# Transfers of weights, values, queries and keys issued at other places of a group and a round; one early sum before small steps; two calls on VectorE moved

## The chip, the cores and the metric

The program runs on one core of a Trainium2 chip. A core has a matrix engine (TensorE, PE in the profile; its weight loads are listed as PEld), a vector engine (VectorE, DVE), a scalar engine (ScalarE, ACT), a general engine (GpSimd, POOL) and a sync engine (SyncE, SP). Each runs its own list of instructions in order, and they wait for one another through semaphores. SP computes nothing: it holds one queue of DMA issues, and an issue whose semaphores have not arrived holds up every issue behind it. ACT and POOL issue some DMAs of their own. The on-chip memory is SBUF, 128 partitions wide; products of PE land in PSUM and are read from there by DVE and ACT. The metric is the device time of one execution in microseconds (us), lower is better.

## The reference

A layer norm of x feeds two branches: a local attention, in which each of 2048 positions looks at itself and at seven earlier ones two apart, and a bilinear feed-forward network. The result is x plus the attention's output times the SiLU of the network's output. In the core of the reference:

```
x = A_x                                     # 1 x 2048 x 640, float32
xn = layernorm(x)
qkv = xn @ wqkv                             # 640 x 1920, 32 heads of 20
idx = pos[:, None] - 2 * arange(8)          # negative ones masked
attn = softmax(einsum(q, k[idx]) * 20**-0.5)
s = einsum(attn, v[idx]) @ wo               # 640 x 640
h = (xn @ w_gate) * (xn @ w_up)             # two 640 x 1536
out = x + s * silu(h @ w_down)              # 1536 x 640
```

## The kernel before

**Products.** Every product keeps float32 accuracy from three passes in a reduced type: each operand is split into a high part (a copy by ACT, L109) and a low part (the operand minus its high part, L110, on POOL unless DVE is named), and PE adds high by high, high by low and low by high. From the feed-forward's column block 3 on, a block of 128 hidden columns is computed for two chunks of 512 positions by seven half-size products in place of eight (a Winograd scheme); the sums and differences that this needs are made on POOL and DVE. `group(f, c0, second)` (L1287) does it for block f and one pair of chunks; its products are called j and come in the order 0, 5, 2, 1, 4, 3, 6 (the place in this order is n). After a product, ACT copies it to SBUF into one of five rotating buffers `gh` (`hold`, L1295); DVE and POOL combine them (L1298 `gate_b`, L1301 `up_b`, L1304 `h_b`, L1308 `gate_a`, L1311 `up_a`), and SP stores two finished tiles h to the DRAM scratch h_scr (L1284). A hold reuses a buffer only once the last reader of it is done: that is L1304 on POOL, or the landing of a store of h.

**The stages.** Up to about 60 us: layer norm, queries, keys and values of the first head groups, first feed-forward blocks. For the norm, `scales` (L278 to L281, L331 to L334, tiny operations on POOL) makes the factors of eight tiles, and PE multiplies them out (L340) for the use by the next transposes; on POOL they stand among `early_sums` (L593), eight sums of 128x512 for the first chunks' Winograd operands, which are stored in t_scr and e_scr and not read before the groups. Up to about 290 us: the remaining queries, keys and values, each stored to qkv_scr by ACT's queue. From 290 to 515 us: two groups for each block, 3 to 10 in f. Then the last block's plain products (`gate`, `up`, L1354 to L1372), and the output projection of the attention: `pair_product` (L1021), seven products again, for pairs of o tiles, which `load_pair` reads from o_scr, `turn_pair` (L976) turns by four 32x32-block transposes (L710, shown as two for each pair) and combines by four sums (L982 to L985), and `hi_pair` (L1008) and `lo_pair` (L1012) split. After 540 us: the down projection and the end.

**The attention** runs on DVE and POOL alone, beside all this, as a generator (`attention`, L461) which yields an estimate of what a step costs and is advanced a little after each product of PE: what stands in which order on an engine is set by these calls and the estimates, in program order. A unit n is one group of heads with one parity of positions. Its 8 offsets are done two at a time (four rounds j = 0, 2, 4, 6): DVE multiplies q by two shifted keys (L527) and sums over the head's columns (L534), and between these, for the unit before, DVE multiplies weights by values (L498) and POOL adds the result up (L504). After the four rounds the sums of the unit before are stored in o_scr by SP (L575), and a softmax of unit n follows (L549 to L563; the exponential is ACT's, L556). Queries (L408), keys and values (L414 and L416, the last ones shifted by a partition) are loaded by SP, keys and values in two alternating buffers `kv`. `ahead(n, parts)` issues the load of unit n's queries and keys (part 0) or of its values (part 1) once, if they have been computed by then.

**SP's queue** is thus shared by the stores of h, the stores of o, the loads of q, keys and values, and the load of a block's raw weights (`load_wf`, L175, 640 KB, in two alternating buffers `wraw`), in program order. Of a block's weights POOL makes the sums (L1272) and the splits (L110) while the block before is multiplied.

Of the kernel before, what the change touches and what calls it, by code (L numbers as in the profile page):

```python
# [43 lines left out]
PAIRS = range(0, W, 2)  # L44
PACE = 1.0
VEC = 3
EARLY = 3
GROUP_RATE = 0.184


# [6 lines left out]
def kernel(  # L57
# [115 lines left out]
    def load_wf(f):  # L173
        wf_raw[f] = slot([P, KD, 2, P], F32) if f == 0 else st([P, KD, 2, P], "wraw", 2)
        nc.sync.dma_start(wf_raw[f], wgu[f])  # L175
# [285 lines left out]
    def attention():  # L461

        def flat(y):
            return y.rearrange("p i c -> p (i c)")

        terms = st([P, 2, NE * CMAX], "t", 2)
        twice = st([P, 2, NE * CMAX], "t", 2)
        spots = NE * W
        m_ps = weights[0:1, CH - spots:].rearrange("p (i w) -> p i w", w=W)
        nc.vector.tensor_copy(m_ps, mask)  # L470
        before, loaded = None, set()

        def ahead(n, parts):

            if n < len(ORDER) and ORDER[n] in made:
                for a in parts:
                    if (n, a) not in loaded and ORDER[n]:
                        loaded.add((n, a))
                        (load_kq if a == 0 else lambda u: load_kv(u, 1))(ORDER[n])

        copied = set()

        def copy_q(n):

            if n not in copied:
                copied.add(n)
                y = flat(q_t[ORDER[n]])
                nc.scalar.activation(q_two[:, :y.shape[1]], y, AF.Copy)

        def values(w):  # L490

            u, e, o = before
            nh = GROUPS[UN[u][0]]
            c = nh * DH
            y = flat(o)
            t = terms[:, w % 2, :NE * c]
            v = flat(kv_t[u][:, 1, w:w + NE, :]).rearrange("p (n d) -> p n d", d=DH)
            nc.vector.tensor_mul(t.rearrange("p (n d) -> p n d", d=DH),  # L498
                                 e[:, :, w].unsqueeze(2).to_broadcast([P, NE * nh, DH]), v)
            eng, cost = (nc.gpsimd, 1.3e-3) if u != ORDER[-1] else (nc.gpsimd, 2.2e-3) if w % 2 else (nc.vector, 2.5e-3)  # L500
            if w == 0:
                return NE * c * cost, lambda: None
            z = terms[:, 0, :NE * c] if w == 1 else y
            return NE * c * cost, lambda: eng.tensor_add(y, z, t)  # L504

        ring[:] = [q_one, "g", "u"]
        for n, u in enumerate(ORDER + [None]):
            if u is not None:
                late_unit = u not in made
                while u not in made:  # L510
                    yield None
                ahead(n, (0, 1))
                for _ in range(5 if late_unit else 0):
                    yield None
                g, r = UN[u]
                nh = GROUPS[g]
                c = nh * DH
                copy_q(n)
                q, kv = q_two[:, :NE * c].unsqueeze(1).to_broadcast([P, 2, NE * c]), kv_t[u]
                lg = st([P, NE * nh, W], "lg", 2)  # L520
                t = twice.rearrange("p a c -> p (a c)")[:, :2 * NE * c].rearrange("p (a c) -> p a c", a=2)
            for j in PAIRS:
                if u is not None:
                    ahead(n + 1, (0,))
                    k = flat(kv[:, 0, j:j + NE, :])
                    k = bass.AP(k.tensor, k.offset, [k.ap[0], [c, 2], k.ap[1]])
                    nc.vector.tensor_mul(t, q, k)  # L527
                    yield 2 * NE * c * 1.22e-3
                if before is not None:
                    cost, add = values(j)  # L530
                    add()
                    yield cost
                if u is not None:
                    nc.vector.tensor_reduce(out=lg[:, :, j:j + 2].rearrange("p n a -> p a n"),  # L534
                                            in_=t.rearrange("p a (n d) -> p a n d", d=DH), op=ALU.add, axis=AX.X)
                    yield 2 * NE * c * 1.2e-3
                if before is not None:
                    cost, add = values(j + 1)
                    add()
                    yield cost  # L540
            if u is None:
                store_o(before)
                ring[:] = three
                return
            ahead(n + 1, (0, 1))
            if before is not None:
                store_o(before)
            m0 = lg[0:1].rearrange("p (i h) w -> p i h w", h=nh)
            nc.vector.tensor_add(m0, m0, m_ps.unsqueeze(2).to_broadcast([1, NE, nh, W]))  # L549
            e = weights[:, :NE * nh * W].rearrange("p (n w) -> p n w", w=W)  # L550
            most = weights[:, CH - spots - NE * nh:CH - spots]
            sm = st([P, 2, NE * nh], "sm", 1)
            nc.vector.tensor_reduce(out=most, in_=lg, op=ALU.max, axis=AX.X)
            nc.vector.tensor_sub(lg, lg, most.unsqueeze(2).to_broadcast([P, NE * nh, W]))
            yield 1.5
            nc.scalar.activation(e, lg, AF.Exp, scale=SCALE)  # L556
            if (n + 1, 0) in loaded:
                copy_q(n + 1)
            finish_piece()
            yield 0.5  # L560
            nc.vector.tensor_reduce(out=sm[:, 0, :], in_=e, op=ALU.add, axis=AX.X)
            nc.vector.reciprocal(sm[:, 1, :], sm[:, 0, :])
            nc.vector.tensor_mul(e, e, sm[:, 1, :].unsqueeze(2).to_broadcast([P, NE * nh, W]))  # L563
            before = u, e, st([P, NE, c], "o", 1)
            yield 1.3
# [42 lines left out]
    def advance(budget):  # L608
        credit[0] += budget
        while running and credit[0] > 0:  # L610
            cost = next(running[0], 0)
            if cost == 0:
                running.pop()
            elif cost is None:
                break
            else:
                credit[0] -= cost
        if credit[0] > 0:
            credit[0] = 0
# [72 lines left out]
    def split_wo(k, eng=nc.gpsimd):  # L692
        y = slot([P, 2, D])
        hi, lo = y[:, 0], y[:, 1]
        split(eng, wo_raw.pop(k), hi, lo)
        wo_s[k] = hi, lo
# [540 lines left out]
    def two(f):  # L1237
        return F_TWO <= f < f1
# [48 lines left out]
    def group(f, c0=0, second=0):  # L1287
# [26 lines left out]
        if not second:  # L1314
            if not two(f - 1):
                w_split(f, "U")
            w_sum.pop(f, None)
            wf_raw.pop(f)
            if f < f1 and f + 1 not in wf_raw:
                load_wf(f + 1)  # L1320
        for n, j in enumerate((0, 5, 2, 1, 4, 3, 6)):
            y = b["ACACABA"[j]]
            runs = [(w_unit(f, H_IN[j], k)[i], x_in(W_IN[j], l, k, c0)) for i, l in ALL3 for k in range(2)]
            if j in FIVE:
                name, ch = FIVE[j]
                runs += [(w_unit(f, name)[i], xT[c0 + ch][l][:, KD - 1, :]) for i, l in ALL3]
            for r, (w, x) in enumerate(runs):
                nc.tensor.matmul(y, w, x, start=j in (0, 1, 5) and r == 0, stop=r == len(runs) - 1,  # L1328
                                 skip_group_check=True)
            if j in (0, 1, 2, 4):  # L1330
                hold(j)
            finish_piece()
            for act in later:
                act()
            later = {5: [gate_a], 3: [gate_b, up_b]}.get(j, [])
            if j == 6:
                unfinished.extend([up_a, h_b])
            if (second, n) in places:
                places[second, n](f)
            if (f, second, n) in beside:  # L1340
                beside[f, second, n]()
            advance(PACE * len(runs) * (GROUP_RATE if two(f) else 0.184))

    places = {}
# [54 lines left out]
    for m, t in ((m, t) for m in range(1, len(MADE)) for t in range(DIL)):  # L1399
# [23 lines left out]
        elif (m, r) == (last, 1):  # L1423
            for k in range(2):
# [3 lines left out]
    w_sum.pop(2)  # L1428
    load_wf(3)
    beside.update({(f0, 0, 5): lambda: advance(1e9), (f0, 1, 0): lambda: begin_last(), (f0, 1, 1): lambda: load_pair(0),  # L1430
                   (f0, 1, 4): lambda: sums_wo(), (f0, 1, 5): lambda: split_wo(0, nc.vector),
                   (f0, 1, 6): lambda: split_wo(1, nc.vector)})

    def begin_last():
        advance(1e9)
# [66 lines left out]
    split_wo(3)  # L1502
    split_w5()
    g3 = gate(f1, 3)
    turn_pair(2)
    up(f1, 3, g3)
    finish_piece()
    begin_wd()
# [23 lines left out]
    for p in range(SP // 2):  # L1532
# [6 lines left out]
        if more:  # L1539
            hi_pair(p + 1, 0)  # L1540
            lo_pair(p + 1, 0)
            if p == 3:
                wd_sums()
        else:
            split_o(SP, y1)
# [129 lines left out]
```

## Time and profile before

| | us |
|---|---|
| median of three runs | 748.99 |
| lowest, highest | 748.61, 751.39 |
| the profiled execution | 748.28 |
| its span | 746.5 |

The profiled execution thus has 1.8 us outside its span, and it ran 0.7 us faster than the median.

| engine | busy us | share of span | instructions |
|---|---|---|---|
| PE | 735.4 | 99% | 4054 |
| DVE | 612.2 | 82% | 720 |
| POOL | 462.6 | 62% | 389 |
| ACT | 302.5 | 41% | 577 |

The rows of a timeline read: start, duration, engine, source line, operation, output<-input, count, and in brackets how long the engine was idle before and what ended that. A row with a count (x2) stands for neighbouring instructions; its duration is theirs together. A row of DMA issues ends with the KB of one and the median time in us from issue to landing. The list of waits names an engine, the bank and line that waited, the engine and line that it waited for, the total in us, how often, and the longest. The table of stretches shows for each engine the busy time and, in brackets, the instructions; then the TensorE clock that was granted, the share of the DMA engines and GB/s.

### The profile page before, as it was taken

What the parts mean: (1) busy time and instruction counts of PE and PEld (TensorE: products, weight loads), DVE (VectorE), ACT (ScalarE), POOL (GpSimd) and SP (SyncE); (2) the same over time, 40 slices, a digit from 0 to 9 for tenths busy, and PEclk for the clock granted to TensorE, in tenths of its full rate; (3) what the DMA queues carried; (4) which work ended last, traced back from release to release, by engine and by line L of the source; (5) the groups of instructions that cost most, each with busy time, mean ns of one, the idle gap of its engine ahead of it and who ended that gap; (6) DMA issues with size and microseconds to landing.
All of it is one profiled execution on the core that took longest, in us unless ns stands there. A gap on an engine that the chain in (4) does not pass through costs nothing. (4 is left out here: it accounts for less than half of the span.)

```text
span 746.5 us, 11102 instructions
## 1 busy us (share of the span) xinstructions
PE 735.4 (99%) x4054; PEld 669.0 (90%) x4054; DVE 612.2 (82%) x720; ACT 302.5 (41%) x577; POOL 462.6 (62%) x389
## 2 busy tenths in 40 slices
PE   8999999999999999999999999999999999999997
PEld 6989989988999998778887888887899999999997
DVE  7666998699697887998999999667998777777775
ACT  5658413323332332233223322335556564444442
POOL 6169929787688878888879989877559800000000
PEclk9999999999999999999999999999999999999999
DMA  9465672947446548856165424268567655555534
GB/s 316 170 202 200 236 224 87 299 157 239 127 152 197 190 128 232 274 161 207 55 159 149 115 82 110 72 178 204 167 177 212 228 220 191 191 191 191 191 106 141
DMA packets 103493, 132.98 MB, mean 178 GB/s; under 512 B 22696, under 2 KB 74404, under 8 KB 103438
## 3 DMA queue, kind: packets, MB, share of 16 engines
q1 hardware_dynamic: 84686, 112.77, 48.4%
q10 hardware_dynamic: 17600, 14.26, 5.9%
q0 software_dynamic: 1152, 5.24, 2.2%
q8 instruction: 32, 0.52, 0.3%
q14 instruction: 23, 0.19, 0.1%
HBM read 83.58 MB, written 47.81 MB: 176 GB/s over the span
## 5 line engine op out<-in xcount | busy, mean ns | idle before, releaser
L504 POOL TENSOR_TENSOR o<-o,t 128x960 f32<-128x960 f32 (+1 forms) x69 | 139.6, 2024 | 19.1 <-DVE t L498 17.6
L498 DVE TENSOR_TENSOR t<-e,kv 128x960 f32<-128x960 f32 (+1 forms) x96 | 99.4, 1037 | 24.8 <-POOL o L504 24.7
L527 DVE TENSOR_TENSOR t<-q,kv 128x1920 f32<-128x1920 f32 (+1 forms) x48 | 92.4, 1925 | 4.3 <-DMA kv<-qkv_scr 4.2
L534 DVE TENSOR_REDUCE lg<-t 128x96 f32<-128x1920 f32 (+1 forms) x48 | 92.3, 1922 | 0.2
L428 PE MATMUL q<-s,xc 128*128 128x360 f32 (+1 forms) x450 | 83.1, 334 | 0.6 <-DVE lg L266 0.5
L110 POOL TENSOR_TENSOR s<-wraw,s 128x384 fp32r<-128x384 f32 (+6 forms) x58 | 69.6, 1210 | 19.9 <-ACT s L109 19.9
L428 PEld LDWEIGHTS q<-s,xc 128*128 128x128 f32 x450 | 74.9, 188 | 4.8 <-DVE lg L266 0.8
L1295 ACT ACTIVATE gh<-g 128x512 f32<-128x512 f32 x54 | 32.2, 597 | 115.8 <-PE g L1328 97.8
L428 PE MATMUL u<-s,xc 128*128 128x360 f32 (+1 forms) x360 | 65.8, 334 | 0.0
L428 PEld LDWEIGHTS u<-s,xc 128*128 128x128 f32 x360 | 60.3, 188 | 2.3
L428 PE MATMUL g<-s,xc 128*128 128x360 f32 (+1 forms) x330 | 61.5, 337 | 0.0
L428 PEld LDWEIGHTS g<-s,xc 128*128 128x128 f32 x330 | 55.7, 188 | 2.6
L1328 PE MATMUL u<-xc,s 128*128 128x512 f32 x216 | 55.3, 391 | 0.9 <-ACT gh L1295 0.9
L896 PE MATMUL q<-xc,s 128*128 128x320 f32 x342 | 55.5, 309 | 0.0
L1328 PE MATMUL g<-s,s 128*128 128x512 f32 x216 | 55.0, 390 | 0.0
L896 PEld LDWEIGHTS q<-xc,s 128*128 128x128 f32 x342 | 51.5, 188 | 0.0
L1328 PEld LDWEIGHTS u<-xc,s 128*128 128x128 f32 x216 | 40.3, 188 | 10.5 <-ACT gh L1295 2.0
L1328 PEld LDWEIGHTS g<-s,s 128*128 128x128 f32 x216 | 40.5, 188 | 8.6 <-ACT gh L1295 0.2
L109 ACT ACTIVATE s<-wraw 128x384 fp32r<-128x384 f32 (+6 forms) x59 | 33.5, 587 | 29.5 <-PE g L1328 9.0
L504 POOL TENSOR_TENSOR o<-t 128x960 f32<-128x960 f32 (+1 forms) x12 | 24.4, 2032 | 31.8 <-DVE t L498 25.2
L1328 PE MATMUL g<-xc,s 128*128 128x512 f32 x168 | 41.5, 391 | 1.3 <-ACT gh L1295 1.3
L119 PE MATMUL g<-xc,s 128*128 128x512 f32 (+1 forms) x180 | 40.1, 373 | 0.0
(367 smaller groups left out, 1566.5 us busy)
## 6 DMA issues: line engine op xcount, KB each, us to landing
h_scr<-gh SPq DMA_DIRECT2D x48, 256.0 KB, 2.6
wraw<-in_wgu SPq DMA_DIRECT2D x11, 640.0 KB, 4.4
kv<-qkv_scr SPq DMA_DIRECT2D x14, 480.0 KB, 5.9
qkv_scr<-s ACTq DMA_DIRECT2D x18, 360.0 KB, 4.4
t<-h_scr SPq DMA_DIRECT2D x8, 768.0 KB, 7.1
kv<-qkv_scr SPq DMA_DIRECT2D x14, 367.5 KB, 6.6
s_scr<-gh SPq DMA_DIRECT2D x16, 320.0 KB, 4.2
gh<-s_scr SPq DMA_DIRECT2D x16, 320.0 KB, 3.5
```

Source lines behind the costliest of these rows:

```text
L109: nc.scalar.activation(hi, raw, AF.Copy)
L110: eng.tensor_sub(lo, raw, hi.bitcast(F32))
L119: nc.tensor.matmul(acc, a, b, start=first and n == 0, stop=last and n == len(runs) - 1)
L428: nc.tensor.matmul(p, xT[(r * NE + i) // TPC][a][:, k, t0:t0 + P], wq[m][b][k], start=n == 0, stop=n == len(runs) - 1, skip_group_check=ac ...
L498: nc.vector.tensor_mul(t.rearrange("p (n d) -> p n d", d=DH), e[:, :, w].unsqueeze(2).to_broadcast([P, NE * nh, DH]), v)
L504: return NE * c * cost, lambda: eng.tensor_add(y, z, t)
L527: nc.vector.tensor_mul(t, q, k)
L534: nc.vector.tensor_reduce(out=lg[:, :, j:j + 2].rearrange("p n a -> p a n"), in_=t.rearrange("p a (n d) -> p a n d", d=DH), op=ALU.add, ax ...
L896: nc.tensor.matmul(p, y[:, i, k], wd_t[name][k][:, l], start=new and r == 0, stop=r == len(runs) - 1, skip_group_check=True)
L1295: nc.scalar.activation(kept[j], b["ACACABA"[j]], AF.Copy)
L1328: nc.tensor.matmul(y, w, x, start=j in (0, 1, 5) and r == 0, stop=r == len(runs) - 1, skip_group_check=True)
```

## The change

Five places are edited.

1. `EARLY` becomes 1: of the eight `early_sums`, one instead of three is issued before the first `scales`. Three follow between the two `scales` as before, and the rest behind.
2. In `attention`, a unit's values are now loaded in the second round (j = 2) of the unit itself, where they were loaded at the end of the unit before; the queries and keys of the unit after are loaded in the third round (j = 4), where they were tried from the first round on. The call at the end of a unit tries part 0 alone. A unit that was waited for ("late") still loads all its parts at once.
3. In `group`, `load_wf` of the next block moves from ahead of the first product of a block's first group to a place behind that product.
4. `split_wo(0)` on DVE moves from the sixth place (n = 5) of a group to the seventh, where `split_wo(1)` is; the group is block 10's second one.
5. `turn_pair(2)` moves from ahead of the last `up` to the first pass of the pair loop, behind `lo_pair(1, 0)`.

```diff
--- before.py
+++ after.py
@@ -44,7 +44,7 @@
 PAIRS = range(0, W, 2)
 PACE = 1.0
 VEC = 3
-EARLY = 3
+EARLY = 1
 GROUP_RATE = 0.184
 
 
@@ -509,7 +509,7 @@
                 late_unit = u not in made
                 while u not in made:
                     yield None
-                ahead(n, (0, 1))
+                ahead(n, (0, 1) if late_unit else (0,))
                 for _ in range(5 if late_unit else 0):
                     yield None
                 g, r = UN[u]
@@ -521,7 +521,10 @@
                 t = twice.rearrange("p a c -> p (a c)")[:, :2 * NE * c].rearrange("p (a c) -> p a c", a=2)
             for j in PAIRS:
                 if u is not None:
-                    ahead(n + 1, (0,))
+                    if j == 2:
+                        ahead(n, (1,))
+                    elif j > 2:
+                        ahead(n + 1, (0,))
                     k = flat(kv[:, 0, j:j + NE, :])
                     k = bass.AP(k.tensor, k.offset, [k.ap[0], [c, 2], k.ap[1]])
                     nc.vector.tensor_mul(t, q, k)
@@ -542,7 +545,7 @@
                 store_o(before)
                 ring[:] = three
                 return
-            ahead(n + 1, (0, 1))
+            ahead(n + 1, (0,))
             if before is not None:
                 store_o(before)
             m0 = lg[0:1].rearrange("p (i h) w -> p i h w", h=nh)
@@ -1316,8 +1319,6 @@
                 w_split(f, "U")
             w_sum.pop(f, None)
             wf_raw.pop(f)
-            if f < f1 and f + 1 not in wf_raw:
-                load_wf(f + 1)
         for n, j in enumerate((0, 5, 2, 1, 4, 3, 6)):
             y = b["ACACABA"[j]]
             runs = [(w_unit(f, H_IN[j], k)[i], x_in(W_IN[j], l, k, c0)) for i, l in ALL3 for k in range(2)]
@@ -1339,6 +1340,8 @@
                 places[second, n](f)
             if (f, second, n) in beside:
                 beside[f, second, n]()
+            if (second, n) == (0, 0) and f < f1 and f + 1 not in wf_raw:
+                load_wf(f + 1)
             advance(PACE * len(runs) * (GROUP_RATE if two(f) else 0.184))
 
     places = {}
@@ -1428,8 +1431,7 @@
     w_sum.pop(2)
     load_wf(3)
     beside.update({(f0, 0, 5): lambda: advance(1e9), (f0, 1, 0): lambda: begin_last(), (f0, 1, 1): lambda: load_pair(0),
-                   (f0, 1, 4): lambda: sums_wo(), (f0, 1, 5): lambda: split_wo(0, nc.vector),
-                   (f0, 1, 6): lambda: split_wo(1, nc.vector)})
+                   (f0, 1, 4): lambda: sums_wo(), (f0, 1, 6): lambda: (split_wo(0, nc.vector), split_wo(1, nc.vector))})
 
     def begin_last():
         advance(1e9)
@@ -1502,7 +1504,6 @@
     split_wo(3)
     split_w5()
     g3 = gate(f1, 3)
-    turn_pair(2)
     up(f1, 3, g3)
     finish_piece()
     begin_wd()
@@ -1539,6 +1540,8 @@
         if more:
             hi_pair(p + 1, 0)
             lo_pair(p + 1, 0)
+            if not p:
+                turn_pair(2)
             if p == 3:
                 wd_sums()
         else:
```

Lines behind L521 stand three higher in the new kernel (L1284 is L1287, L1012 is L1015).

**SP's queue between the groups of blocks 5 and 6 (about 379 to 392 us).** The first piece is the kernel before, the second the changed one; h_scr<-gh is a store of h, kv and q are loads for the attention, o_scr<-o a store of its sums, wraw<-in_wgu the load of a block's weights. In the kernel before, the load of weights stands two rows above the first row shown.

```order
L1284 DMA h_scr<-gh_3349 128x4x128
L414 DMA kv_124<-qkv_scr_2086 128x960
L416 DMA kv_124<-qkv_scr_2086 112x840
L416 DMA kv_124<-qkv_scr_2086 15x840
L575 DMA o_scr<-o_3163 128x8x80
L575 DMA o_scr<-o_3163 128x8x40
L408 DMA q_3468<-qkv_scr_2463 128x960
L414 DMA kv_1029<-qkv_scr_2463 128x960
L416 DMA kv_1029<-qkv_scr_2463 112x840
L416 DMA kv_1029<-qkv_scr_2463 15x840
L1284 DMA h_scr<-gh_3415 128x4x128
L1284 DMA h_scr<-gh_3447 128x4x128
```

```order
L1287 DMA h_scr<-gh_3349 128x4x128
L175 DMA wraw_3419<-in_wgu 128x1280
L578 DMA o_scr<-o_3159 128x8x80
L578 DMA o_scr<-o_3159 128x8x40
L1287 DMA h_scr<-gh_3413 128x4x128
L1287 DMA h_scr<-gh_3444 128x4x128
L414 DMA kv_124<-qkv_scr_2086 128x960
L416 DMA kv_124<-qkv_scr_2086 112x840
L416 DMA kv_124<-qkv_scr_2086 15x840
L408 DMA q_3592<-qkv_scr_2455 128x960
L414 DMA kv_1029<-qkv_scr_2455 128x960
```

The load of weights has come behind the two stores of h of the group before, and the stores of o and the next two stores of h have come ahead of the six loads of values and keys and of the load of q.

**DVE at the end of block 10's second group (about 502 to 507 us, when PE is already at block 11's group).** Before, then after. L939 (L942) is the last sum for wo, L110 the low parts of wo's first two blocks of rows, L1298 (L1301) the group's `gate_b` and L1311 (L1314) its `up_a`.

```order
L939 TENSOR_TENSOR o_4296<-t_4242,kv_4259 128x640
L110 TENSOR_TENSOR s_4312<-t_4239,s_4312 128x640
L1298 TENSOR_TENSOR gh_4270<-gh_4270,u_4225 128x512
L110 TENSOR_TENSOR s_4329<-t_4239,s_4329 128x640
L1311 TENSOR_TENSOR gh_4232<-gh_4232,g_4224 128x512
```

```order
L942 TENSOR_TENSOR o_4296<-t_4242,kv_4259 128x640
L1301 TENSOR_TENSOR gh_4270<-gh_4270,u_4225 128x512
L110 TENSOR_TENSOR s_4326<-t_4239,s_4326 128x640
L110 TENSOR_TENSOR s_4329<-t_4239,s_4329 128x640
L1314 TENSOR_TENSOR gh_4232<-gh_4232,g_4224 128x512
```

`gate_b` now stands ahead of both low parts, and `up_a` directly behind both, as before.

**DVE where the output projection begins (about 527 to 535 us).** Before, then after. L797 and L800 (L800 and L803) are sums for the down projection, L1012 (L1015) the low part of a half of pair 1, L1039 and L1042 (L1042 and L1045) read products of pair 0 from PSUM.

```order
L710 STREAM_TRANSPOSE s_4525<-s_4459 128x640 x2
L982 TENSOR_TENSOR s_4459<-s_4525 128x256
L983 TENSOR_TENSOR s_4459<-s_4459,s_4525 128x256
L984 TENSOR_TENSOR s_4459<-s_4525,s_4459 128x256
L985 TENSOR_TENSOR s_4525<-s_4525 128x256
L797 TENSOR_TENSOR lg_4567<-wraw_4494 128x320
L800 TENSOR_TENSOR lg_4568<-wraw_4494,lg_4567 128x320
L1012 TENSOR_TENSOR xc_4552<-s_4483,xc_4552 128x640
L1039 TENSOR_TENSOR gh_4599<-o_4554,u_4571 128x320
L1042 TENSOR_TENSOR gh_4611<-o_4554,q_2_66 128x320
```

```order
L800 TENSOR_TENSOR lg_4560<-wraw_4494 128x320
L803 TENSOR_TENSOR lg_4561<-wraw_4494,lg_4560 128x320
L1015 TENSOR_TENSOR xc_4545<-s_4483,xc_4545 128x640
L713 STREAM_TRANSPOSE s_4574<-s_4459 128x640 x2
L985 TENSOR_TENSOR s_4459<-s_4574 128x256
L986 TENSOR_TENSOR s_4459<-s_4459,s_4574 128x256
L987 TENSOR_TENSOR s_4459<-s_4574,s_4459 128x256
L988 TENSOR_TENSOR s_4574<-s_4574 128x256
L1042 TENSOR_TENSOR gh_4599<-o_4547,u_4564 128x320
L1045 TENSOR_TENSOR gh_4611<-o_4547,q_2_66 128x320
```

The two transposes and four sums of pair 2 now stand behind the low part of pair 1 and directly ahead of the two reads of pair 0's products. The order on PE is the same in both kernels.

## Prediction

> **What bounds the kernel now.** I read the page, then PE's waits, then the table of stretches, then what releases each wait.
>
> ```profile
> PE 735.4 (99%) x4054; PEld 669.0 (90%) x4054; DVE 612.2 (82%) x720; ACT 302.5 (41%) x577; POOL 462.6 (62%) x389
> ```
>
> PE is busy 99% of the span, and its instructions and their order are the same in both kernels. The change can give or take only PE's waiting.
>
> ```profile
> PE g L1328 <- ACT gh L1295: 1.3, 2, 0.9
> PE e L340 <- POOL lg L334: 1.0, 1, 1.0
> PE u L1328 <- ACT gh L1295: 0.9, 2, 0.6
> PE e L1033 <- DVE xc L1012: 0.8, 1, 0.8
> ...
> PE q L1033 <- DVE gh L1042: 0.2, 1, 0.2
> ```
>
> These are seven waits: two of 0.9 and 0.4, one of 1.0, two of 0.6 and 0.3, then 0.8 and 0.2; 4.2 us together, all that the change could touch here.
>
> ```profile
> 300.00:315.00 15.00, 14.91 (x65) 11.70 (x64) 14.41 (x20) 4.19 (x7) 12.14 (x14) 1.00 0.81 256
> ...
> 420.00:435.00 15.00, 15.00 (x68) 12.25 (x67) 14.30 (x16) 6.58 (x11) 11.84 (x9) 1.00 0.62 173
> ```
>
> The granted clock is 1.00 in both. An undisturbed stretch holds 68 matmuls, so one costs 15.00 / 68 = 0.22 us. The stretch from 300 lost three, 0.66 us, and the list has no wait for them: small delays beside the listed ones are real.
>
> **Part 1, the early sums.**
>
> ```profile
> 43.79 2.55 POOL L593 TENSOR_TENSOR kv<-xc 128x512 f32<-128x512 f32 x2 [17.92 <-DVE xc L370]
> 47.55 0.21 POOL L278 TENSOR_TENSOR lg<-lg 128x4 f32<-128x4 f32 x1
> ...
> 45.02 0.17 DVE L277 RECIPROCAL lg<-lg 128x4 f32<-128x4 f32 x1
> ```
>
> `scales` had its input at 45.02 + 0.17 = 45.19 but began on POOL at 47.55, behind three sums. With one sum (2.55 / 2 = 1.28) POOL is free at 45.07, so `scales` begins near 45.2, 2.3 us earlier, and the wait of 1.0 at L340 goes: **-1.0**. The two sums run behind it and the stores of the sums come a little later; nothing reads those before the groups. If that cover were gone it would cost the two sums, 2.6.
>
> **Parts 2 and 3, SP's queue.** The wait of 0.4 at L1328 is at 323.
>
> ```profile
> 314.95 1.98 SPq L1284 DMA_DIRECT2D h_scr<-gh  x2
> ...
> h_scr<-gh SPq DMA_DIRECT2D x2, 256.0 KB, 7.4
> ...
> 322.88 0.60 ACT L1295 ACTIVATE gh<-g 128x512 f32<-128x512 f32 x1 [2.60 <-PE u L1328]
> ```
>
> The hold at 322.88 is shown behind PE, which had long been done; its buffer is freed by the first store of 314.95, which takes 7.4 us, to 322.4. Ahead of it on SP stand the values of unit 8 and the queries and keys of unit 9; they now come behind it. Landing a few us sooner takes the wait away: **-0.4**, and nothing at worst.
>
> The wait of 0.9 ends with the hold at 398.25.
>
> ```profile
> 379.77 3.39 SPq L1284 DMA_DIRECT2D h_scr<-gh  x2
> ...
> 386.12 3.53 SPq L408 DMA_DIRECT2D q<-qkv_scr  x1
> ...
> 391.27 0.93 SPq L1284 DMA_DIRECT2D h_scr<-gh  x2
> ...
> wraw<-in_wgu SPq DMA_DIRECT2D x11, 640.0 KB, 4.4
> ...
> 398.25 0.60 ACT L1295 ACTIVATE gh<-g 128x512 f32<-128x512 f32 x1 [2.98 <-DMA h_scr<-gh]
> ...
> 384.92 0.77 POOL L1272 TENSOR_TENSOR wraw<-wraw 128x256 f32<-128x256 f32 x1
> ...
> 392.59 2.26 POOL L504 TENSOR_TENSOR o<-t 128x960 f32<-128x960 f32 x1 [5.39 <-DMA o_scr<-o]
> ```
>
> The same: the store issued at 391.27 lands just before 398.25, 7 us later, and the hold follows. The queue was held by the loads of 386.12 and after; in the changed order the store is ahead of them all. The listed wait goes: **-0.9** (0 at worst). The 5.39 that POOL waits for the store of o should shorten too, but PE doesn't wait for it.
>
> Against this stands the load of weights: it stood ahead of the two stores of 379.77 and is now behind them, at 383.2. With the median of 4.4 it lands at 387.6, while POOL's sums began at 384.92: POOL waits up to 2.7, in front of an idle time of 5.39. It costs nothing here; without that cover POOL's chain of splits would be 2.7 late. In the other rounds the first sum comes later after the stores, and I cost them at nothing.
>
> Around 280 the load of weights of block 3 goes ahead of the values of unit 7.
>
> ```profile
> 284.45 0.73 POOL L1272 TENSOR_TENSOR wraw<-wraw 128x256 f32<-128x256 f32 x1 [2.48 <-DMA wraw<-in_wgu]
> ```
>
> POOL waited 2.48 for it and then works without a longer pause into the stretch from 300; it starts earlier, and the splits and gates there with it. I give this half of the 0.66 lost there, **-0.3** (0 to -0.66). The 0.3 among the waits for u at L1328 is the same chain: half, **-0.15**.
>
> The tight place is unit 8.
>
> ```profile
> 278.93 0.54 SPq L408 DMA_DIRECT2D q<-qkv_scr  x1
> 295.39 1.19 SPq L1284 DMA_DIRECT2D h_scr<-gh  x2
> ...
> kv<-qkv_scr SPq DMA_DIRECT2D x1, 480.0 KB, 9.8
> kv<-qkv_scr SPq DMA_DIRECT2D x1, 367.5 KB, 12.4
> ...
> 307.46 2.15 DVE L527 TENSOR_TENSOR t<-q,kv 128x1920 f32<-128x1920 f32 x1
> ```
>
> Its q and keys were issued at 278.93 and now come behind the two stores of 295.39, so near 296 to 297.5. The keys' two large parts took 9.8 and 12.4 then, beside loads of POOL's that are done by 296. With 9.8 they would land at 306 to 307.3, just before DVE wants them at 307.46. I take that, the nearer row without those loads, and cost it at nothing, with no reserve.
>
> **Part 4, `gate_b` ahead of two low parts.**
>
> ```profile
> 504.03 0.81 DVE L110 TENSOR_TENSOR s<-t,s 128x640 fp32r<-128x640 f32 x1
> 504.77 0.68 DVE L1298 TENSOR_TENSOR gh<-gh,u 128x512 f32<-128x512 f32 x1
> 505.37 0.81 DVE L110 TENSOR_TENSOR s<-t,s 128x640 fp32r<-128x640 f32 x1
> 506.10 0.68 DVE L1311 TENSOR_TENSOR gh<-gh,g 128x512 f32<-128x512 f32 x1
> ...
> 505.58 1.75 POOL L1304 TENSOR_TENSOR gh<-gh,gh 128x512 f32<-128x512 f32 x1 [2.15 <-issue]
> ...
> 509.10 0.60 ACT L1295 ACTIVATE gh<-g 128x512 f32<-128x512 f32 x1 [1.14 <-DMA h_scr<-gh]
> ...
> 510.19 1.98 PE L1328 MATMUL g<-xc,s 128*128 128x512 f32 x8
> ```
>
> Here PE's 0.6 arises: L1298, L1304, then the hold for which PE waits. With L1298 at 504.03, L1304 can begin 0.7 earlier. But operations of DVE with both inputs in SBUF, as L110, wait for POOL's current one (next fence). L1304, freed at 504.7, runs between the two L110: the first ends at 505.45, L1304 (about 1.25 without its wait) at 506.7, the second at 507.4, then L1311 at 508.05, 1.25 later than 506.78. Its store must land before the hold at 509.10, which moves to 510.35; PE, which began the product behind it at 510.19, can do so at 510.35 + 0.60 = 510.95: **+0.75**, the 0.6 being hidden by it. Without the exclusion the 0.6 goes and L1311 stays: -0.5.
>
> **Part 5, the pair turned later.**
>
> ```profile
> 525.12 1.67 DVE L984 TENSOR_TENSOR t<-s,t 128x256 f32<-128x256 f32 x1
> 529.32 0.42 DVE L982 TENSOR_TENSOR s<-s 128x256 f32<-128x256 f32 x1
> 534.22 0.47 DVE L1042 TENSOR_TENSOR gh<-o,q 128x320 f32<-128x320 f32 x1
> ...
> 527.48 1.49 POOL L1373 TENSOR_TENSOR gh<-gh,gh 128x512 f32<-128x512 f32 x1
> ...
> 532.10 1.12 POOL L110 TENSOR_TENSOR kv<-wraw,kv 128x320 fp32r<-128x320 f32 x1
> 533.18 1.44 POOL L110 TENSOR_TENSOR xc<-lg,xc 128x320 fp32r<-128x320 f32 x1
> ```
>
> The same four sums take 1.67 each beside POOL and 0.42 with POOL idle: an operation of either engine runs whole, and then the other's. Now: L797 waits for L1373 to 528.97, L800 follows, L1012 ends at 530.7 (PE's 0.8 goes), the transposes, which POOL did not slow in this trace, end at 532.2. The first sum then waits for POOL to 533.1 and ends at 533.5; POOL's last L110 runs to 534.55; the second sum ends at 535.0, the other two at 535.8, L1039 at 536.2 and L1042 at 536.6 instead of 534.69. The next product of PE waits for that: **+1.9**. Without the exclusion L1042 would end at 533.7: **-1.0**. I take +1.9, since three of the four sums beside POOL took some 1.67.
>
> The Trainium skill, page "SBUF — State Buffer", section "Who interferes with whom", says that a DVE instruction with two SBUF inputs contends with a GpSimd one that reads SBUF, and that whoever issues first has the port for the whole instruction. It speaks against parts 4 and 5, as the rows do. It names no turn-taking: if DVE's four sums went through in one piece once they had the port, L1042 would end at 535.8, +1.1, and the sum below would be 747.4 instead of 748.2.
>
> **The sum.** -1.0 (part 1), -0.4, -0.9, -0.3, -0.15 (parts 2 and 3: -1.75), +0.75 (part 4), +1.9 (part 5): -0.1 on a profiled execution of 748.28, so 748.2. The median of the runs, 748.99, stands 0.7 above that execution; the sum is kept as it is. From 540 us on PE shows no waits in the list, so a shift passes to the end.
>
> **Rivals.**
> - *The exclusion costs little in parts 4 and 5*, because POOL's operations fall elsewhere once both engines shift: 748.28 - 2.75 - 0.5 - 1.0 = 744.0. For it: DVE's place depends on PE and POOL's on ACT, and 1 us of relative shift leaves the sums alone with idle POOL. Against it: both are tied to the same products. 0.28.
> - *The stores of h stay slow*, because POOL's own loads and not SP's fill the DMA engines: parts 2 and 3 give nothing, 748.28 - 1.0 + 0.75 + 1.9 = 749.9. For it: the share of DMA in the stretch from 300 is 0.81, and SP's order doesn't change what is moved. 0.15.
> - *Slower: the keys of unit 8 land late.* If they take 12.4 us as the slowest did (the part of 367.5 KB), they land at 309.7 to 310: DVE is 2.5 late where it has hardly a pause (14.41 of 15 us busy), the gates behind it and PE follow, and the 0.85 of that stage is lost: 748.2 + 2.5 + 0.85 = 751.55. It decides from a landing at 307.5 on. 0.13.
>
> **Chances and range.** The forecast (746.7 to 749.7) has 0.44. Half a per cent, 3.7 us, is what a measurement of this kernel tells from no change: faster than 745.25 is the first rival, 0.28 (with a before of 748.99); slower than 752.7 needs the third and more, 0.10; 0.62 is left. The range reaches from the first rival to the third, 743.8 to 751.6.
>
> **What would show it.** Part 1: no wait of PE at L340, `scales` near 45.2. Parts 2 and 3: the two stores land in under 5 us, PE's waits at 323 and 397 are gone. Part 4: POOL's h_b between the two low parts and PE waiting for a hold near 510. Part 5: sums of 1 us and more near 533, PE waiting for L1045. I am wrong if the sums there take 0.42, if L530 (the first round's product of keys) of unit 8 waits for a DMA, or if POOL waits for weights longer than 3 us.

## The result and the profile after

The changed kernel takes 751.11 us (median; 749.79 to 755.82), the kernel before, run beside it, 749.15 (747.52 to 751.39). The ratio is 1.0028, with an interval of 1.0017 to 1.0039: slower by 0.3%, some 2 us. It lies within the range and within the half per cent called "no change", but in the other direction than forecast: -0.1 us was forecast for a profiled execution, 748.28 to 748.2, and the profiled execution took 750.83.

The page of the changed kernel, and its list of waits of PE:

```profile
span 749.1 us, 11099 instructions
PE 735.2 (98%) x4054; PEld 670.2 (89%) x4054; DVE 615.0 (82%) x720; ACT 302.4 (40%) x577; POOL 463.5 (62%) x389
```

```profile
PE g L1329 <- ACT gh L1298: 2.5, 1, 2.5
PE u L119 <- ACT pk L441: 2.2, 1, 2.2
PE q L1036 <- DVE gh L1045: 2.2, 1, 2.2
...
```

(L1329 is L1328 of the kernel before: between the two edits of `group` the line numbers are one higher, not three.)

PE's work is what it was (735.2 us against 735.4). The seven waits of before, 4.2 us in all, are gone from the list, and three new ones of 2.2 to 2.5 us have come, 6.9 us in all. (One of 0.7, at L307, lies in the first 20 us, ahead of all that was edited.) The difference, 2.7, is near the 2.6 by which the span grew, but that is not the whole account: small losses that no list shows went as well, and a slower clock came (below). The table of stretches shows the gain of parts 2 and 3, in the columns stretch, PE (matmuls), PEld, DVE, ACT, POOL, granted clock, DMA and GB/s. The kernel before first, then the changed one:

```profile
315.00:330.00 15.00, 14.53 (x64) 11.70 (x63) 15.00 (x13) 4.69 (x8) 12.05 (x11) 1.00 0.68 180
390.00:405.00 15.00, 14.13 (x63) 11.38 (x62) 14.65 (x13) 4.69 (x8) 12.41 (x9) 1.00 0.57 156
```

```profile
300.00:315.00 15.00, 15.00 (x68) 12.43 (x67) 14.03 (x20) 3.90 (x7) 10.88 (x12) 1.00 0.95 311
315.00:330.00 15.00, 15.00 (x68) 12.43 (x67) 15.00 (x13) 5.10 (x9) 14.24 (x13) 1.00 0.74 212
390.00:405.00 15.00, 15.00 (x68) 12.43 (x67) 15.00 (x13) 5.00 (x9) 13.62 (x10) 1.00 0.68 208
```

All three of the changed kernel hold the 68 matmuls of an undisturbed stretch; before, the first held 65, the other two 64 and 63. The two stores of h near 315 us, as the view of DMA issues shows them:

```profile
h_scr<-gh SPq DMA_DIRECT2D x2, 256.0 KB, 2.3
```

They took 7.4 us from issue to landing before, and 2.3 now.

**The new wait near 88 us.** A row of ACT, one of SP and one of the chain that ended last:

```profile
89.83 0.47 ACT L441 ACTIVATE pk<-g 128x360 f32<-128x360 f32 x1 [9.02 <-DMA t_scr<-t]
...
84.61 0.32 SPq L607 DMA_DIRECT2D t_scr<-t  x1
...
84.61 4.53 DMA t_scr<-t
```

In the kernel before, the rows of the same work were these:

```profile
86.00 0.47 ACT L441 ACTIVATE pk<-g 128x360 f32<-128x360 f32 x1 [3.82 <-DMA t_scr<-t]
...
83.14 0.32 SPq L604 DMA_DIRECT2D t_scr<-t  x1
```

ACT's store of qkv (L445), ahead of L441 in its list, waits until SP's store in t_scr, issued at 84.61, has landed. Both use the same DMA semaphore, as the lists of instructions of the changed kernel show, though the one reads nothing that the other writes: the store in t_scr raises the semaphore to 112 when it has landed, and L445 waits for 112. The kernel before has the same pair.

```
SP   L607 DMA t_scr<-t_70 128x512 [waits DMAHW1_49,Pool_49]
ACT  L445 DMA qkv_scr_767<-s_794 384x1x240 [waits DMAHW1_49,Activation_49]
```

Before, that cost ACT 3.8 us of idle time and PE nothing. Now the store is issued 1.5 us later, since two of the early sums were put off, and it takes 4.5 us instead of 2.2. So L441 is 3.7 later, PE has come 1.4 earlier, and PE waits for the PSUM tile that L441 empties. Why the store takes 2.3 longer no run shows. With two early sums instead of one it takes 2.5 (`e1_two`, below).

**The new wait near 508 us** (rows of DVE, POOL and SP, the DMA issue, ACT):

```profile
501.59 0.68 DVE L1301 TENSOR_TENSOR gh<-gh,u 128x512 f32<-128x512 f32 x1
502.19 3.42 DVE L110 TENSOR_TENSOR s<-t,s 128x640 fp32r<-128x640 f32 x2
505.54 0.68 DVE L1314 TENSOR_TENSOR gh<-gh,g 128x512 f32<-128x512 f32 x1
...
503.06 1.87 POOL L1307 TENSOR_TENSOR gh<-gh,gh 128x512 f32<-128x512 f32 x1
504.88 0.60 POOL L1189 DMA_DIRECT2D xc<-e_scr  x1
...
506.24 0.93 SPq L1287 DMA_DIRECT2D h_scr<-gh  x2
...
h_scr<-gh SPq DMA_DIRECT2D x2, 256.0 KB, 3.9
...
510.08 0.60 ACT L1298 ACTIVATE gh<-g 128x512 f32<-128x512 f32 x1 [4.51 <-DVE gh L1311]
```

The two low parts take 1.7 each, not 0.81, beside POOL. POOL's h_b (L1307) is early, and right behind it POOL issues its load of xc, 1.4 us ahead of the store of h; before, it issued it 0.5 behind that store. The store takes 3.9 us instead of 2.2. The hold that waits for it is thus 1.0 later than before (510.08 instead of 509.10), while PE reaches the product behind it 1.9 earlier (508.27 instead of 510.19); before, the hold had been done 0.5 ahead of PE.

**The new wait near 534 us** (rows of POOL, DVE and PE, then two stretches):

```profile
531.66 0.89 POOL L110 TENSOR_TENSOR xc<-wraw,xc 128x320 fp32r<-128x320 f32 x1 [1.45 <-ACT xc L109]
532.50 0.89 POOL L110 TENSOR_TENSOR kv<-wraw,kv 128x320 fp32r<-128x320 f32 x1
533.34 1.06 POOL L110 TENSOR_TENSOR xc<-lg,xc 128x320 fp32r<-128x320 f32 x1
...
532.81 0.86 DVE L985 TENSOR_TENSOR s<-s 128x256 f32<-128x256 f32 x1
533.71 0.98 DVE L986 TENSOR_TENSOR s<-s,s 128x256 f32<-128x256 f32 x1
534.72 0.43 DVE L987 TENSOR_TENSOR s<-s,s 128x256 f32<-128x256 f32 x1
535.79 0.48 DVE L1045 TENSOR_TENSOR gh<-o,q 128x320 f32<-128x320 f32 x1
...
536.33 1.33 PE L1036 MATMUL q<-xc,kv 128*128 128x320 f32 x6 [2.17 <-DVE gh L1045]
...
536.00:538.00 2.00, 1.67 (x9) 1.68 (x10) 2.00 (x4) 0.00 (x0) 0.00 (x0) 0.78 0.00 0
538.00:540.00 2.00, 2.00 (x9) 2.00 (x9) 1.08 (x3) 0.77 (x2) 0.00 (x0) 0.50 0.47 163
```

Two of the four sums take twice their 0.42 beside POOL, and the second read ends at 536.27. Behind the wait the granted clock is 0.78 and then 0.50: each of these stretches of 2 us has nine matmuls, where the kernel before, at a clock of 1.00, has 14 and 16.

### The profile page after: what moved, and what is told of

Read it like the earlier page. It is cut to its first block, busy times and chain, and to the rows that moved or that the text cites. A ratio compares the mean times of both kernels' runs of the same rounds, so it can differ in the third digit from the quotient of the medians.

```text
span 749.1 us, 11099 instructions
## 1 busy us (share of the span) xinstructions
PE 735.2 (98%) x4054; PEld 670.2 (89%) x4054; DVE 615.0 (82%) x720; ACT 302.4 (40%) x577; POOL 463.5 (62%) x389
## 4 chain that ended last, share of the span: by engine, by line
PE 87%; POOL 4%; DVE 3%; DMA 3%; SPq 1%; issue 1%; ACT 1%; ACTq 0%; DVEq 0%; POOLq 0%
PE g L1329 14%; PE q L428 9%; PE u L1329 9%; PE q L899 8%; PE u L428 8%; PE g L428 7%; PE u L899 6%; PE q L1329 5%; PE g L119 4%; PE u L119 3%; PE g L899 3%; PE e L899 3%; PE q L119 2%; POOL kv L596 2%; PE q L1036 1%; PE u L1036 1%
## 5 line engine op out<-in xcount | busy, mean ns | idle before, releaser
L110 POOL TENSOR_TENSOR s<-wraw,s 128x384 fp32r<-128x384 f32 (+6 forms) x58 | 70.4, 1224 | 24.0 <-ACT s L109 24.0
L1298 ACT ACTIVATE gh<-g 128x512 f32<-128x512 f32 x54 | 32.3, 598 | 114.6 <-PE g L1329 103.4
L1329 PE MATMUL u<-xc,s 128*128 128x512 f32 x216 | 55.3, 391 | 0.0
L1329 PE MATMUL g<-s,s 128*128 128x512 f32 x216 | 54.8, 389 | 0.0
L1329 PEld LDWEIGHTS u<-xc,s 128*128 128x128 f32 x216 | 40.3, 188 | 9.6 <-ACT gh L1298 1.1
L1329 PEld LDWEIGHTS g<-s,s 128*128 128x128 f32 x216 | 40.6, 188 | 8.4
L1329 PE MATMUL g<-xc,s 128*128 128x512 f32 x168 | 41.4, 391 | 2.5 <-ACT gh L1298 2.5
L119 PE MATMUL u<-xc,s 128*128 128x512 f32 (+1 forms) x180 | 40.1, 373 | 2.2 <-ACT pk L441 2.2
```

Of the source, the lines that this page charges most:

```text
L110: eng.tensor_sub(lo, raw, hi.bitcast(F32))
L119: nc.tensor.matmul(acc, a, b, start=first and n == 0, stop=last and n == len(runs) - 1)
L1298: nc.scalar.activation(kept[j], b["ACACABA"[j]], AF.Copy)
```

## The experiments

Each kernel ran beside the kernel before, and a ratio is to that, with its 95% interval in brackets; 0.001 of it is 0.75 us.

### Each part by itself

```diff
-EARLY = 3
+EARLY = 1
```

> Part 1 alone. Theory (from the changed kernel's trace): the two early sums put off delay POOL's high and low parts and so the stores in t_scr by about 1.5 us; ACT's store of qkv (L445) waits for one of these stores, and PE waits about 2 us for L441 near 88 us. Then the wait of 1.0 us at L340 goes and one of 2.0 to 2.4 us comes at L119: a profiled execution 1.0 to 1.4 us slower than before. Rival: the wait near 88 us comes from parts 2 and 3 (SP's other order); then part 1 alone is 1.0 us faster and has no wait near 88 us.

Measured: 750.55 us, ratio 1.0018 (1.0005 to 1.0030). Its waits of PE, and the stretch behind the first:

```profile
PE u L119 <- ACT pk L441: 2.1, 1, 2.1
PE g L1328 <- ACT gh L1295: 1.8, 2, 1.5
...
90.70:94.70 4.00, 3.98 (x11) 3.15 (x12) 3.93 (x3) 2.37 (x4) 2.23 (x1) 0.60 1.07 391
```

The wait near 88 us belongs to part 1, and the ratio, 1.3 us slower, is within what was expected: the theory holds. (SP's order from parts 2 and 3 isn't in this kernel.) The profile shows more: behind the wait of 2.1 PE's clock was 0.60 for 4 us, and the wait at 325 us, 0.4 before, became 1.5, since the stores of h stayed slow there (8.4 us).

Parts 2 and 3 together are the two hunks of `attention` and the two of `group`.

> Parts 2 and 3 alone. Theory: the stores of h land sooner, and of PE's excess over its pace the 0.4, 0.6 and 0.5 us between 300 and 345 and the 1.0 near 398 go, with 0.3 to 0.6 new between 330 and 425: 1.7 to 2.3 us faster than before (0.9970 to 0.9977), the wait at L340 stays, no wait near 88 us. Rival: without part 1's shift the transfers meet others and give at most half of it; a second rival, that they bring the wait near 88 us, gives 0 or slower.

Measured: 746.05 us, 0.9958 (0.9944 to 0.9972); the runs lie between 745.67 and 746.19, those of the kernel before between 746.6 and 750.9. The gain is 3.1 us, above what was expected; PE is busy throughout every stretch of 15 us between 300 and 405 us.

Part 4:

```diff
-                   (f0, 1, 4): lambda: sums_wo(), (f0, 1, 5): lambda: split_wo(0, nc.vector),
-                   (f0, 1, 6): lambda: split_wo(1, nc.vector)})
+                   (f0, 1, 4): lambda: sums_wo(), (f0, 1, 6): lambda: (split_wo(0, nc.vector), split_wo(1, nc.vector))})
```

> Part 4 alone. Theory from the changed kernel's trace: POOL's h_b is done earlier, so POOL issues its load of xc from e_scr ahead of the store of up_a, which is later by the exclusion of DVE and POOL; the store takes 3.7 us instead of 2.2 and PE waits near 2.5 us for the hold behind it: 1.7 to 1.9 us slower. Rival, the prediction's: only the exclusion counts, the store takes 2.2 us, 0.75 us slower.

Measured: 750.33 us, 1.0022 (1.0012 to 1.0032), 1.6 us slower: the theory. PE's wait for the hold is 2.4 us, and the store took 4.0; behind the wait the clock fell:

```profile
PE g L1328 <- ACT gh L1295: 3.7, 3, 2.4
...
511.40:515.00 3.60, 3.06 (x8) 2.41 (x9) 2.45 (x4) 2.06 (x4) 1.80 (x2) 0.62 0.85 187
```

Part 5 moves `turn_pair(2)` as the change does.

> Part 5 alone. Theory (the prediction's): the four sums alternate with POOL's low parts, the second read of pair 0's product ends 1.5 to 2 us later than before and PE waits for it about 2.2 us instead of 1.0: 1.9 us slower, of which a part is PE's slower clock behind the wait (0.6 of full in the changed kernel). Rival: what the changed kernel lost there came from the shift of the engines by the other parts; alone it gains 0.5 to 1.0 us.

Measured: 750.70 us, 1.0017 (1.0005 to 1.0029).

```profile
PE q L1033 <- DVE gh L1042: 2.2, 1, 2.2
...
537.00:541.00 4.00, 4.00 (x20) 4.00 (x21) 2.58 (x5) 1.56 (x4) 0.00 (x0) 0.65 0.32 104
```

The wait of 2.2 instead of 1.0 is part 5's own, not one of shifted engines; 20 matmuls in the 4 us behind it, instead of 27 before, add to it in this execution. Over all runs it cost 1.3 us, less than the 1.9 expected, which the interval (0.4 to 2.2) still holds.

The four changes add up to 1.0015 where the whole change has 1.0028. Each has an interval of some 0.0012 on either side, so this doesn't show that the parts cost more together than apart.

### What is in the wait of part 4

Part 4 as above, and POOL's load of xc issued earlier, ahead of the last `sums_wo`:

```diff
-    (f1, 0, 5): sum_w5,
-    (f1, 0, 3): lambda: load_e(3, 0, 2)})
+    (f1, 0, 5): sum_w5})
-                   (f0, 1, 4): lambda: sums_wo(),
+                   (f0, 1, 4): lambda: (load_e(3, 0, 2), sums_wo()),
```

> Part 4, and POOL's load of xc from e_scr, which part 4 alone issues just ahead of the store of up_a, issued a few us earlier (behind the low parts of the block's weights). Theory: with the load out of the way the store lands in 2.2 us instead of 3.7 and PE's wait behind it shrinks from 2.4 to 0.8 to 1.2 us: 0.5 to 1.0 us slower than before, with no slower clock of PE behind the wait. Rival: the store is slow for another reason or late enough by the exclusion alone; the wait stays at 2 us or more, 1.5 us slower.

Measured: 749.63 us, 1.0005 (0.9995 to 1.0016). The two stores of h, and the holds that PE waits for:

```profile
h_scr<-gh SPq DMA_DIRECT2D x2, 256.0 KB, 2.3
...
PE g L1328 <- ACT gh L1295: 3.1, 3, 1.2
```

With the load out of the way the store takes 2.3 again, and PE's wait for the hold is 1.2 instead of 2.4. So about half of part 4's wait is POOL's load in front of the store. What is left, 0.4 us with an interval from -0.4 to 1.2, holds both the 0.75 of the prediction and nothing at all.

### Two early sums

```diff
-EARLY = 3
+EARLY = 2
```

> Two early sums ahead of the first scales, where the kernel before has three and part 1 one; nothing else. Theory: scales then begin near 46.4 and end near 48.2, just before PE wants them, so at most 0.2 of the wait of 1.0 at L340 is left; the stores in t_scr come no later than before, so PE has no wait of over 1 us near 88 us: 0.8 to 1.0 us faster than before. Rival: any shift of PE ahead of POOL's stores brings the wait near 88 us back, since ACT's store of qkv waits for a store in t_scr in any order; then 0.5 to 1.5 us slower.

Measured: 748.79 us, 1.0000 (0.9990 to 1.0011). PE's waits:

```profile
PE g L1328 <- ACT gh L1295: 2.2, 2, 1.5
PE q L224 <- POOL lg masks.py:199: 1.4, 1, 1.4
PE u L1328 <- ACT gh L1295: 0.9, 2, 0.6
```

The wait at L340 is gone and none came near 88 us, so the rival falls; but nothing was gained, so the theory's 0.8 to 1.0 falls too. The hold at 322.88, for which PE waited 0.4, is now at 322.15 and waited for 1.5: PE reaches the product behind it 1.7 us earlier, and the store of h lets the hold come only 0.7 earlier. That a gain ahead of that place is given back there as long as the stores are slow was not in the prediction.

### Part 2 and part 3 apart

> Part 2 alone. Theory: it is the loads of values, q and keys behind the stores of h and o that free these stores, so most of the gain of parts 2 and 3 together (3.0) is here: PE's waits near 323 and 398 us are gone, 2 to 3 us faster than before. Rival: the load of weights ahead of the stores is as much in the way; then part 2 alone gives 1.5 or less and part 3 the rest.

Measured: 745.78 us (745.08 to 745.88), 0.9956 (0.9942 to 0.9970). The two stores of h near 313 us took 2.3.

> Part 3 alone. Theory: the load of weights comes 3.5 to 4.5 us later, POOL waits for it beside other idle time, and the stores of h that PE waits for still stand behind the loads of values, q and keys: within 0.7 us of the kernel before, waits near 323 and 398 us as before. Rival: 1 us or more faster, with one of these waits gone.

Measured: 751.68 us, 1.0036 (1.0024 to 1.0047). The stores at 314 us, the waits and the stretch behind the first:

```profile
h_scr<-gh SPq DMA_DIRECT2D x2, 256.0 KB, 9.3
...
PE g L1326 <- ACT gh L1295: 3.4, 2, 1.9
...
323.50:327.50 4.00, 3.34 (x8) 2.69 (x9) 4.00 (x4) 1.74 (x3) 4.00 (x4) 0.60 0.01 3
```

All of the gain is part 2's. Part 3 by itself makes the kernel slower, 2.7 us, which neither the theory nor the rival had: the stores take 9.3 instead of 7.4, and waits of 0.4 and 0.9 became 1.9 and 1.5. Why they take longer there was not tried. Beside part 2 it changes nothing that can be measured (0.9958 with it, 0.9956 without).

### Without parts 4 and 5

> Parts 1, 2 and 3 (the changed kernel without parts 4 and 5). Theory: the gain of parts 2 and 3 stays, and part 1 takes its wait of 1.0 away and brings the wait of about 2.2 us near 88 us, with PE's clock at times slower behind it: 1.0 to 1.8 us slower than parts 2 and 3 alone, 1.2 to 2.0 us faster than before; parts 4 and 5 then cost 3 to 4 us together. Rival: with the transfers spread, the stores in t_scr land sooner and the wait near 88 us is under 1 us; then it is as fast as parts 2 and 3 alone.

Measured: 746.71 us (745.92 to 749.34), 0.9974 (0.9962 to 0.9987). The wait near 88 us is 2.0, and against parts 2 and 3 alone (0.9958) part 1 costs 0.0016, 1.2 us, as expected. From here to the changed kernel (1.0028) parts 4 and 5 cost 0.0054, 4.0 us.

### The pair still later, and versions that could beat both

```diff
-    turn_pair(2)
     up(f1, 3, g3)
...
         if p == 0:
+            turn_pair(2)
             load_pair(4)
```

> The pair turned behind both reads of pair 0's products (behind the product j = 5) instead of ahead of them as in part 5. Theory: the low part of pair 1 is no longer behind the four sums and the sums no longer ahead of the reads, so PE's waits of 0.8 and 0.2 near 533 us go and none comes before 546 us: 1.0 to 1.5 us faster than before. Rival: the four sums then delay the low parts of pair 1 that follow, and PE waits for these: between 0.5 us faster and 1 us slower.

Measured: 749.02 us, 0.9997 (0.9986 to 1.0009). The waits of 0.8 and 0.2 near 533 us are gone, and in their place PE loses four times 0.3 to 0.4 between 543 and 565 us, waiting for ACT's copies (L1036) among others. It is as fast as before, so the time is the rival's.

The next kernel has parts 2 and 3, `EARLY = 2`, this place of the pair, and both low parts of wo behind `up_a`:

```diff
-                   (f0, 1, 5): lambda: split_wo(0, nc.vector),
-                   (f0, 1, 6): lambda: split_wo(1, nc.vector)})
+                   })
...
-    beside.update({(f1, 0, 0): lambda: (turn_pair(0), load_pair(1)),
+    beside.update({(f1, 0, 0): lambda: (split_wo(0, nc.vector), split_wo(1, nc.vector), turn_pair(0), load_pair(1)),
```

> Parts 2 and 3 with two early sums, the pair turned behind both reads, and both low parts of wo behind gate_b and up_a. Theory: the gains add up, 2.3 to 3 of the transfers, 0.9 of the early sums, 1.0 to 1.5 of the pair and 0.5 to 1.0 of the low parts, since gate_b and up_a no longer stand behind operations that wait for POOL: 4.7 to 6.4 us faster than before, 0.9915 to 0.9937. Rival: the stages meet each other's shifts and half is lost, 0.9955.

Measured: 745.87 us, 0.9955 (0.9942 to 0.9969): the rival. The wait near 505 us is gone, but 1.0 came at L119 near 88 us, where ACT waits for the store in t_scr (4.0 us here), and the short waits behind 533.

```profile
PE e L1036 <- ACT o L1039: 1.1, 2, 0.7
PE u L119 <- ACT pk L441: 1.0, 1, 1.0
...
PE e L1036 <- DVE gh L1045: 0.4, 1, 0.4
```

The last has parts 2 and 3 and only the low parts behind `up_a`.

> Parts 2 and 3, and both low parts of wo behind gate_b and up_a; three early sums and the pair as before. Theory: of PE's losses of parts 2 and 3 alone the 1.2 us near 505 go, and nothing new comes, since neither PE nor POOL is shifted before 505 us: 1.0 to 1.2 us faster than parts 2 and 3 alone, 3.8 to 4.2 us faster than before (0.9944 to 0.9950). Rival: DVE's chain behind 505 us is 1.5 us later by the two low parts, and PE waits for it near 530 us instead: as fast as parts 2 and 3 alone.

Measured: 746.10 us, 0.9959 (0.9945 to 0.9973): the rival again. The wait near 505 us is gone, but for the low part of a pair (L1015) PE now waits 1.7 instead of 0.8, with a slower clock behind it:

```profile
PE e L1036 <- DVE xc L1015: 1.7, 1, 1.7
...
531.50:534.00 2.50, 2.26 (x8) 2.00 (x9) 2.50 (x5) 0.00 (x0) 0.62 (x1) 0.63 0.24 60
```

Part 2 alone, 745.78 us, beats both kernels and is the simplest of those that do; three others cannot be told from it.

## Why the prediction was wrong

Most of its mechanisms came as described, but three of its four terms lie outside what was measured, and one of these, part 1, had the wrong sign. Each part by itself, in us of the 749:

| part | forecast | measured alone | interval |
|---|---|---|---|
| 1 | -1.0 | +1.3 | 0.4 to 2.2 |
| 2 and 3 | -1.75 | -3.1 | -4.2 to -2.1 |
| 4 | +0.75 | +1.6 | 0.9 to 2.4 |
| 5 | +1.9 | +1.3 | 0.4 to 2.2 |

- **Part 1, "-1.0", with the cover named as "nothing reads those before the groups".** This is the step that failed. `scales` began at 45.19, as said, and the wait at L340 went. But a store need not be read to be waited for: ACT's next DMA takes the semaphore of one of the stores in t_scr, and PE waits 2.2 for what ACT does behind it. The row that gave it away was in the trace of before: ACT idle for 3.82 us on t_scr<-t at 86.00. PE didn't wait for it then, because L441 was done at 86.97 and PE's next product began at 89.70, a cover of 2.7 us; PE came 1.4 earlier and L441 3.7 later, which is more than the cover. The 2.6 that the prediction gave for a lost cover was meant for the two sums themselves; that the miss, 2.3, came out near it is luck.
- **Parts 2 and 3, "-1.75".** Right in mechanism and too small. The stores land in 2.3 instead of 7.4, and not only the listed waits but the small losses of that stage are gone. The forecast was costed against one profiled execution. PE's wait near 323 was 0.4 in that one and up to 1.5 in other kernels with that order of SP, so the other executions of the kernel before may lose more than that one did; this isn't shown. Part 3's share, told as harmless, is nothing beside part 2, and 2.7 us slower alone.
- **The keys of unit 8, the slower rival.** It did not come: DVE's first product of the unit began at 307.52, as against 307.46 before, and waited for no load. POOL waited 2.58 for the weights at 386.93, within the 2.7 given, and PE did not.
- **Part 4, "+0.75".** The alternation of the two low parts with POOL's h_b came as described. The step left out the DMA that POOL issues behind h_b: moved earlier with it, it stood in front of the store of h, and with that load out of the way the time fell from 1.6 to 0.4 us above the kernel before. Whether the 0.75 itself is right the runs can't tell.
- **Part 5, "+1.9".** The wait came for the operation and the reason told; its size did not. The end of the second read, 536.27, looks near the 536.6 of the working, but PE and POOL were some 0.7 us later there than before, so the read is 0.9 later against PE, not 1.9. Two sums were held up, to 0.86 and 0.98 and not to 1.67, and POOL's three low parts beside them were shorter too (0.89, 0.89 and 1.06 instead of 1.17, 1.12 and 1.44). PE waited 2.2 where it had waited 1.0, so 1.2: nearer the +1.1 that the prediction worked out for sums that go through in one piece. The 1.3 measured excludes neither. The Trainium skill, page "SBUF — State Buffer", section "Who interferes with whom", has a DVE instruction with two SBUF inputs contend with a GpSimd one that reads SBUF. This trace agrees: the two sums beside POOL's low parts took 0.86 and 0.98, the last two, with POOL idle, 0.43 and 0.42.
- **A term that it doesn't have: the clock.** The prediction priced each wait at its length, while PE's clock fell behind most waits of about 2 us (last section). As an estimate from the mean clocks given there, 0.9961 for the changed kernel and 0.999 for the kernel before, 0.003 of clock over 749 us of a PE that is nearly always busy is some 2 us, as much as the change lost in all.
- **The rival of 744.0**, that the exclusion costs little, asked for gains in both places, and both parts made the kernel slower. **The rival of slow stores** is refuted by the 2.3.

## What to carry to other kernels

An operation that only delays a DMA which nobody reads soon can still be on a path, if another queue's DMA uses the same semaphore: look in the trace for an engine that is idle for a DMA it has no business with, and count the cover behind it before the work ahead of it is moved. When a step moves, the DMAs behind it in its engine's list move too, and here a load that came in front of a store cost the store's landing 1.7 us. In this kernel a gain ahead of a place where PE waits for slow stores was given back at that place: free the transfer first. And measure the parts one at a time: here one part of five held the whole gain.

## What the runs showed of the hardware

**PE's clock after a wait.** Behind waits of PE of about 2 us, the granted clock fell to between 0.50 and 0.66 for some 2.5 to 4 us and came back by itself: after 2.1 near 88 us with part 1 alone (0.60), 1.9 near 322 with part 3 alone (0.60), 2.4 near 509 with part 4 alone (0.62), 2.2 near 534 with part 5 alone (0.65), 2.0 near 88 with parts 1 to 3 (0.66), and 1.7 near 530 in the last kernel (0.63). Behind shorter waits, up to 1.5, no profile shows it. The mean clock over all runs of a kernel goes the same way: 0.9961 for the changed kernel, 0.9975 to 0.9984 for the six with a wait of 1.7 us or more in the profile, 0.9990 to 0.9997 for the kernel before and the six whose waits are all shorter. It isn't certain that the waits do it: no run holds the waits and changes the clock, and in the changed kernel's profile the clock was 1.00 behind the waits of 2.2 near 88 us and 2.5 near 508, and fell only behind the third. In the stretch of part 1 alone PE did 11 matmuls in 4.0 us, where 18 of 0.22 us fit at full clock: 1.5 us lost beside the 2.1 of the wait. So a wait of nearly 2 us or more can cost much more than its length; it may also be why the changed kernel's runs reach from 749.79 to 755.82, while part 2 alone, whose longest wait is 1.4, stays within 0.8 us (this link was not tried). The Trainium skill, page "TensorE: Matmul & The Clock Gate", section "What's actually happening", tells of a gate that halves the clock after an idle window of about 3.4 us and restores it after a busy one. The half (0.50 from 538 to 540 us) and the length of the dip agree; the idle times here were shorter than that window.

**Transfers in one queue.** A store of h, 256 KB, took 2.3 us with none of SP's loads of values, queries and keys just ahead of it, 3.9 to 4.0 behind one load of POOL's, and 6.3 to 9.3 behind those loads of SP's. Part 2 changed only the places of these loads in SP's order, and took the stores near 315 us from 7.4 to 2.3.
